# A gate in front of two more head pairs' loads, in a block-sparse attention kernel with a feed-forward layer

## Chip, cores, metric

One Trainium2 chip, one core. The metric is device time of one execution in microseconds (us), the median of several executions. Times within a trace count from the span's start.

## The reference

Attention with a block mask over 4 batches, 8 heads, 768 positions, head size 64, then a layer that multiplies two projections, and two matrices behind it:

```python
scores = scale * np.matmul(q, k.transpose(0, 1, 3, 2))
# mask: neighbours, first and last block, three sampled blocks per row of blocks
scores = np.where(mask, scores, -1000000000.0)
attn = np.exp(scores - np.max(scores, axis=-1, keepdims=True))
attn = attn / (np.sum(attn, axis=-1, keepdims=True) + 1e-09)
attn_out = np.matmul(attn, v)
x = np.ascontiguousarray(attn_out.transpose(0, 2, 1, 3)).reshape(B * S, H * D)
a = x @ w1;  b = x @ w2
out = ((a * b) @ w3) @ w_out
```

Inputs and output are float32.

## The kernel before

The program is planned on the host: a list scheduler (`plan.run()`) with estimated costs puts all tasks in an order, and each engine then runs its own tasks in that fixed order. q, k and v come in by loads that GpSimd issues and that cast to bfloat16. One load carries one of the three for a pair of heads: 192 KB as written.

```python
def load(name, out_of, src, writes, deps=()):
    seq[0] += 1
    t = add(name, {POOL: 0.73}, lambda t: nc.gpsimd.dma_start(out=out_of(), in_=src),
            deps=deps, writes=writes, kind="load", prio=seq[0])
    ...                                     # cut: costs for the scheduler

def load_pair(b, pr, which):
    for tag, src in (("qn", qv), ("kn", kv), ("vn", vv)):
        if tag[0] in which:
            key = (tag, b, pr)
            LD[key] = load(f"ld {key}", lambda key=key: T(*key), src[b][:, 2 * pr:2 * pr + 2],
                           [key], gate(b, pr))
```

The work of attention is cut into 48 units: a batch, a third of the rows, a pair of heads. Batch 0 has units 0 to 11; batch 1 does its pairs 0 and 1 in units 12 to 17 and its pairs 2 and 3 from unit 18 on. A gate is a copy of one element per partition on GpSimd that reads the reciprocal (`rec`) of the unit `lead` = 9 places ahead. GpSimd runs in order, so all loads behind the gate wait too.

```python
def gate(b, pr):
    at = next(i for i, u in enumerate(units) if u[0] == b and u[2] // 2 == pr // 2) - int(PRM["lead"])
    if b < 2 or at < 0:
        return ()
    if at not in GATE:
        ...                                 # cut: names
        GATE[at] = add(f"gate {at}", {POOL: 0.2}, lambda t, rk=rk: nc.gpsimd.tensor_copy(
            gate_sb, T(*rk)[:, 0, 0]), reads=[rk], prio=seq[0])
    return (GATE[at],)
```

For pairs 2 and 3 of batch 1, VectorE copies q and k to another layout (`qs`) and v to a wider tile, and SyncE transposes `qs` by DMA. SyncE's queue also transposes the attention output (`x`) and two blocks of w3 (`w3t`). These transposes and the loads share 16 DMA engines, in two queues: "software" for what GpSimd issues, "hardware" for what SyncE and ScalarE issue.

The softmax here doesn't subtract the row's maximum and nothing guards it: scores larger than these inputs give would overflow.

## Time and profile before

| | before |
|---|---|
| median of the three runs | 244.33 us (244.26 to 244.6) |
| span of the profiled run, granted clock of TensorE | 242.7 us, 1.00 |
| busy: TensorE, ScalarE, VectorE, GpSimd | 98%, 77%, 72%, 18% |
| the six loads concerned: issued, landed | 40.6 to 48.7 us, 57.0 to 64.0 us |
| their first reader, their last reader | 64.2 us, 71.6 us |

A load has three times: its issue on GpSimd, its landing, and the start of its reader. The timeline of GpSimd shows only the first, the DMA view the second (as time since the issue), the timeline of the reading engine the third. The free time between landing and reader is called slack here.

### The profile page before, as it was taken

Reading aid. Unit: us, or ns where it says so; the run is one execution under the profiler, and the core shown is the slowest. Engines: PE = TensorE matmul, PEld = TensorE weight load, DVE = VectorE, ACT = ScalarE, POOL = GpSimd, SP = SyncE. Lnnn points to the kernel's source line nnn. Section 1 sums busy time; section 2 is a strip of 40 time slices with the busy share of each in tenths; the row PEclk is TensorE's granted clock in tenths of the full one; section 3 lists DMA queues with packets and bytes.
Section 4 is the critical chain, followed back from the end, with each engine's and each line's share of the span. In section 5 each row is a group of like instructions: output and inputs, shape, how many; then the busy total and the mean of one; then the engine's idle time right before and its main releaser. Section 6 shows DMA issues by size and latency. Waiting matters only on the chain.

```text
span 242.7 us, 6332 instructions
## 1 busy us (share of the span) xinstructions
PE 237.5 (98%) x2651; PEld 137.8 (57%) x2651; DVE 175.3 (72%) x319; ACT 186.3 (77%) x239; POOL 44.4 (18%) x74
## 2 busy tenths in 40 slices
PE   8999999999999999999999999999999999999995
PEld 7466666667655555555555555554555544444583
DVE  6999898887998787787889778987776831143041
ACT  4898989999889798999899899899989532332341
POOL 9852443410016000700240070000000000000000
PEclk9999999999999999999999999999999999999999
DMA  7999999999869971999199479910024121300312
GB/s 168 182 204 208 207 189 164 193 174 168 121 87 175 174 99 23 113 219 203 58 160 136 111 97 222 201 38 1 26 63 154 24 43 43 130 0 4 130 43 89
DMA packets 52898, 29.39 MB, mean 121 GB/s; under 512 B 32645, under 2 KB 48901, under 8 KB 52869
## 3 DMA queue, kind: packets, MB, share of 16 engines
q0 software_dynamic: 16832, 14.29, 40.9%
q1 hardware_dynamic: 35348, 14.23, 30.3%
q10 hardware_dynamic: 688, 0.46, 0.6%
q8 instruction: 21, 0.34, 0.6%
q14 instruction: 9, 0.07, 0.1%
HBM read 29.36 MB, written 6.29 MB: 147 GB/s over the span
## 4 chain that ended last, share of the span: by engine, by line
PE 91%; DVE 5%; DMA 2%; POOL 1%; issue 0%; POOLq 0%
PE f L748 35%; PE f L774 17%; PE o L665 15%; PE s L639 15%; PE f L728 6%; DMA kn<-in_k_dram 2%; DVE mask L343 1%; DVE e L651 1%; PE f L716 1%; PE f L584 1%; DVE qkt L343 1%; DVE qs L343 1%; POOL qn L379 0%; POOL hotf L414 0%; DVE w3t L343 0%
## 5 line engine op out<-in xcount | busy, mean ns | idle before, releaser
L645 ACT ACTIVATE e<-s 128x1024 bf16<-128x1024 f32 x144 | 140.9, 1025 | 13.5 <-PE s L639 13.1
L748 PE MATMUL f<-x,w 128*128 128x512 bf16 (+1 forms) x448 | 93.7, 349 | 0.0
L651 DVE TENSOR_TENSOR e<-e,mask 128x2048 bf16<-128x2048 bf16 x72 | 87.5, 1219 | 4.9 <-ACT e L645 4.3
L759 DVE TENSOR_TENSOR big<-f,a 128x512 bf16<-128x512 f32 (+1 forms) x56 | 34.2, 612 | 34.5 <-PE f L748 25.5
L748 PEld LDWEIGHTS <-w 128*128 128x128 bf16 x448 | 39.4, 98 | 31.7 <-issue 4.4
L665 PEld LDWEIGHTS <-e 128*128 128x128 bf16 x1152 | 44.6, 97 | 19.9 <-DVE e L651 5.0
L665 PE MATMUL o<-v,e 128*128 128x65 bf16 x1152 | 50.5, 194 | 0.5 <-DVE xn L678 0.5
L756 ACT CAST a<-f 128x512 bf16<-128x512 f32 (+1 forms) x56 | 29.5, 529 | 22.7 <-PE f L748 22.7
L774 PE MATMUL f<-wf,big 128*128 128x512 bf16 (+2 forms) x208 | 46.6, 363 | 0.0
L639 PE MATMUL s<-qkt 64*128 64x256 bf16 x576 | 44.5, 272 | 0.3 <-DVE qkt L343 0.3
L639 PEld LDWEIGHTS <-qkt 64*128 64x128 bf16 x576 | 22.1, 94 | 22.0 <-issue 18.3
L774 PEld LDWEIGHTS <-big 128*128 128x128 bf16 x208 | 17.9, 98 | 17.6 <-issue 1.9
L343 ACT COPY ob<-f 128x512 f32<-128x512 f32 (+1 forms) x20 | 11.6, 578 | 13.1 <-PE f L774 13.1
L678 DVE TENSOR_TENSOR xn<-o,rec 128x256 bf16<-128x256 f32 x48 | 20.3, 423 | 1.2
L673 DVE RECIPROCAL rec<-o 128x4 f32<-128x4 f32 x48 | 8.6, 180 | 16.8 <-PE o L665 16.7
L728 PE MATMUL f<-wo,w3t 128*128 128x512 bf16 x64 | 17.3, 380 | 0.0
L458 POOL COPY gate<-rec 128x1 f32<-128x1 f32 x4 | 0.8, 189 | 76.4 <-DVE rec L673 76.4
L379 POOL DMA_DIRECT2D vn<-in_v_dram x16 | 11.4, 714 | 3.5 <-DVE rec L673 1.0
L379 POOL DMA_DIRECT2D qn<-in_q_dram x15 | 10.9, 725 | 3.5 <-issue 1.6
L379 POOL DMA_DIRECT2D kn<-in_k_dram x15 | 10.8, 717 | 4.1 <-DMA vn<-in_v_dram 1.9
L480 PE MATMUL o<-zero 128*128 128x128 bf16 (+2 forms) x51 | 6.7, 303 | 1.1 <-POOL zero L477 1.1
L728 PEld LDWEIGHTS <-w3t 128*128 128x128 bf16 x64 | 4.9, 98 | 4.3 <-issue 1.7
(64 smaller groups left out, 91.5 us busy)
## 6 DMA issues: line engine op xcount, KB each, us to landing
out_dram<-ob SPq DMA_DIRECT2D x23, 256.0 KB, 2.2
vn<-in_v_dram POOLq DMA_DIRECT2D x16, 192.0 KB, 8.9
qn<-in_q_dram POOLq DMA_DIRECT2D x15, 192.0 KB, 6.3
kn<-in_k_dram POOLq DMA_DIRECT2D x15, 192.0 KB, 7.2
big<-in_moe_w_dram POOLq DMA_DIRECT2D x8, 256.0 KB, 12.0
w<-in_moe_w_dram POOLq DMA_DIRECT2D x4, 512.0 KB, 13.8
wo<-in_moe_w_out_dram POOLq DMA_DIRECT2D x2, 512.0 KB, 11.5
q<-in_q_dram SPq DMA_DIRECT2D x2, 192.0 KB, 3.4
```

Of the source, the lines that this page charges most:

```text
L343: (nc.scalar.copy if t.eng == ACT else nc.vector.tensor_copy)(out, in_)
L379: t = add(name, {POOL: 0.73}, lambda t: nc.gpsimd.dma_start(out=out_of(), in_=src), deps=deps, writes=writes, kind="load", prio=seq[0])
L639: nc.tensor.matmul(s[:, h, k2 * QT:(k2 + 1) * QT], lhsT=z[64 * h:64 * h + 64, 1, kc * 128:(kc + 1) * 128], rhs=z[64 * h:64 * h + 64, 0, t3 ...
L645: exps.append(add(f"E {m} {j}", {ACT: 0.915}, lambda t, sk=sk, ek=ek, j=j: nc.scalar.activation(T(*ek)[:, j], T(*sk), AF.Exp, scale=1.0 / ...
L651: tm = add(f"K {m}", {DVE: 1.137}, lambda t, ek=ek, t3=t3, pick=pick: nc.vector.tensor_tensor(T(*ek), T(*ek), mask[:, t3, pick, :].unsquee ...
L665: nc.tensor.matmul(o[:, qt, h, :], lhsT=e[:, j, h, lo:lo + 128], rhs=w[:, h, kc, :], start=kc == 0 and qt == 0 and h == 0, stop=kc == C - ...
L678: tx = add(f"xn {rk}", {DVE: 0.342}, lambda t, rk=rk, ok=ok, xk=xk, pr=pr: nc.vector.tensor_tensor(T(*xk)[:, :, 128 * pr:128 * pr + 128].r ...
L728: nc.tensor.matmul(T(*key), lhsT=T("w3t", i)[:, j, :], rhs=wo_sb[:, j, :], start=j == 0, stop=j == NF - 1)
L748: nc.tensor.matmul(T(*key)[:, :nt], lhsT=w[:, c, f * 128:(f + 1) * 128], rhs=T(*xk)[:, c, :nt], start=c == 0, stop=c == 3)
L756: ta = add(f"a {i}{f}", {ACT: 0.06 + 0.43 * r}, lambda t, ak=ak, key=ends["w1"][0], nt=nt: nc.scalar.copy(T(*ak)[:, :nt], T(*key)[:, :nt]) ...
L759: nc.vector.tensor_tensor(T(*hk)[:, 512 * (f % 2):512 * (f % 2) + nt], T(*key)[:, :nt], T(*ak)[:, :nt], op=ALU.mult),
L774: nc.tensor.matmul(T(*key)[:, :width], lhsT=T(*hk[f // 2])[:, at:at + 128], rhs=wf_sb[:, f, cols], start=f == 0, stop=f == NF - 1)
```

## The change

The loads of the last two pairs of batch 1 had no gate; batches 2 and 3 have one for each two pairs. The change gives these six loads a gate as well, so that fewer transfers are in flight while weights and transposes compete for the DMA engines.

```diff
-        if b < 2 or at < 0:
+        if b == 0 or b == 1 and pr < 2 or at < 0:
             return ()
```

## The prediction

> **What bounds the kernel now.** I read the page of the kernel before first: the busy shares, then the chain of work that ended last.
>
> ```profile
> span 242.7 us, 6332 instructions
> PE 237.5 (98%) x2651; PEld 137.8 (57%) x2651; DVE 175.3 (72%) x319; ACT 186.3 (77%) x239; POOL 44.4 (18%) x74
> PE 91%; DVE 5%; DMA 2%; POOL 1%; issue 0%; POOLq 0%
> ```
>
> TensorE is busy for 237.5 of 242.7 us and is 91% of the chain that ended last. The 5.2 us that it isn't busy lie before 30 us (8.40 of 10, 9.63 of 10 and 9.84 of 10 us busy in the first three stretches of ten) and after the last matmul. In every stretch between 40 and 90 us, where the change acts, TensorE is busy without a break. DMA in the chain is one load at 3 us. So a change of load times can move the end only if it makes TensorE wait where it doesn't now, or removes a wait that the busy bars hide. I looked for both.
>
> The second view is the timeline of GpSimd, which issues all loads that cast. Columns: start, duration, engine, line, operation, tile, count, then in brackets the idle time before and what ended it.
>
> ```profile
> 39.16 0.74 POOL L379 DMA_DIRECT2D w<-in_moe_w_dram  x1 [0.58 <-DMA qn<-in_q_dram]
> 40.56 0.70 POOL L379 DMA_DIRECT2D qn<-in_q_dram  x1 [0.66 <-DMA kn<-in_k_dram]
> 43.18 0.72 POOL L379 DMA_DIRECT2D kn<-in_k_dram  x1 [1.93 <-DMA vn<-in_v_dram]
> 44.62 0.72 POOL L379 DMA_DIRECT2D vn<-in_v_dram  x1 [0.72 <-DMA big<-in_moe_w_dram]
> 45.97 0.72 POOL L379 DMA_DIRECT2D qn<-in_q_dram  x1 [0.63 <-PE f L584]
> 47.55 0.72 POOL L379 DMA_DIRECT2D kn<-in_k_dram  x1 [0.86 <-PE f L748]
> 48.72 0.72 POOL L379 DMA_DIRECT2D vn<-in_v_dram  x1 [0.46 <-DVE e L651]
> 71.76 0.22 POOL L458 COPY gate<-rec 128x1 f32<-128x1 f32 x1 [22.32 <-DVE rec L673]
> ```
>
> The six q, k, v lines from 40.56 to 48.72 are the loads of pairs 2 and 3 of batch 1, exactly those that the change gates. The line at 39.16 is the load before them, the second half of w2. The line at 71.76 is the first gate as it exists now, for batch 2. The six loads are not free today either: each is held until the eighth load before it has landed. So the software queue is kept eight deep.
>
> The third view gives the landing time, taken over a window that holds one issue at a time (last column: us from issue to landing): w1's second half, w2's second half, then q, k, v of pair 2 and q, k, v of pair 3.
>
> ```profile
> w<-in_moe_w_dram POOLq DMA_DIRECT2D x1, 512.0 KB, 14.6
> w<-in_moe_w_dram POOLq DMA_DIRECT2D x1, 512.0 KB, 16.3
> ...
> qn<-in_q_dram POOLq DMA_DIRECT2D x1, 192.0 KB, 16.4
> kn<-in_k_dram POOLq DMA_DIRECT2D x1, 192.0 KB, 15.1
> ...
> vn<-in_v_dram POOLq DMA_DIRECT2D x1, 192.0 KB, 16.4
> qn<-in_q_dram POOLq DMA_DIRECT2D x1, 192.0 KB, 15.6
> kn<-in_k_dram POOLq DMA_DIRECT2D x1, 192.0 KB, 15.2
> vn<-in_v_dram POOLq DMA_DIRECT2D x1, 192.0 KB, 15.3
> ```
>
> Adding these to the issue times gives landings at 52.4 (w1, issued at 37.82), 55.5 (w2), 57.0, 58.3, 61.0, 61.6, 62.8 and 64.0 us. They come in issue order and one behind the other: w2 takes 3.1 us behind w1, and the six loads take 8.5 us together, 1.4 us each. A load of 192 KB that finds a short queue takes much less from issue to landing: the first one behind the gate at 71.76 took 5.0 us. So of the 15 to 16 us some 10 are time in line. That line is the fact that decides this case.
>
> The fourth view is the timeline of VectorE around the consumers.
>
> ```profile
> 48.71 0.17 DVE L673 RECIPROCAL rec<-o 128x4 f32<-128x4 f32 x1
> ...
> 64.17 0.33 DVE L596 COPY qs<-qn 128x768 bf16<-128x768 bf16 x1
> ...
> 66.16 0.36 DVE L609 COPY v<-vn 128x768 bf16<-128x768 bf16 x1
> ...
> 71.60 0.34 DVE L609 COPY v<-vn 128x768 bf16<-128x768 bf16 x1
> ```
>
> The reciprocal at 48.71 is the tenth of the kernel; it is the one that the new gate reads. The three copies are the first, third and last readers of the six loads; the others are at 64.75, 69.24 and 69.51. None shows idle time waiting for a load. Slack now: 64.17 - 57.0 = 7.2 us for q of pair 2, 64.75 - 58.3 = 6.4 for k, 66.16 - 61.0 = 5.2 for v, 69.24 - 61.6 = 7.6, 69.51 - 62.8 = 6.7 and 71.60 - 64.0 = 7.6 for pair 3.
>
> **What the Trainium skill says.** "DMA: Bandwidth & Descriptors", section "Queues, rings and completion order": each DMA engine takes turns between queue rows at packet granularity, and within a row "descriptors are consumed in ring order". The landings above agree: eight loads, one order. The consequence is that a load cannot slow one that stands ahead of it in its own row; it can only take turns with the other rows, here the transposes that SyncE issues. The same page, section "Issuing engines are not separate DMA queues", says that both kinds run on the same engines; the trace agrees, since a transpose of weights issued at 44.27 took 16.7 us to land, against 3 to 4 us for transposes issued from 64.5 on. "Perfetto Trace Analysis", section "Summary: the profiler window per engine type", says that the slice of a GpSimd DMA leaves out the data movement: 0.72 us on the timeline against 15 to 16 us to landing, so the timeline of GpSimd alone would mislead. "Advanced Engine Details and Errata", section "Mode Summary", says that GpSimd and VectorE share a port and can block each other. That would matter because six issues move. The trace doesn't show it at this size: the mask multiply at 42.43, which the issue at 43.18 overlaps, took 1.22 us, and the one at 50.06, where GpSimd is idle, took 1.22 us too.
>
> **The change part by part.** The gate for this pair of loads is the unit 9 places ahead of unit 18, the first unit that needs them: unit 9, the tenth of 12 in batch 0. The order of instructions, compared between both kernels, is the same on TensorE, VectorE, ScalarE and SyncE; GpSimd has one more instruction, a copy of one element per partition, ahead of the six loads.
>
> Removed: the six separate waits for landings, by then long satisfied (the last load waited for had landed at 34.74 + 13.4 = 48.1 us), and VectorE's waits ahead of the v loads.
>
> Added: one gate copy of about 0.2 us (0.22 in the row at 71.76), on an engine that is 18% busy, and one wait on VectorE before the reciprocal two units later, at 54.98, because the reciprocal's two buffers rotate. The gate will be done by about 49.2, so this costs only the extra semaphore instruction of 0.02 us.
>
> Moved: the reciprocal ends at 48.88. By the gate at 71.76 (reciprocal 71.51, copy 71.76, first load 72.24) the first load follows a reciprocal's start by 0.73 us, so q of pair 2 is issued at about 49.4 and the rest follow 0.72 us apart: 50.2, 50.9, 51.6, 52.3, 53.0. The delays are 8.9, 7.0, 6.3, 5.6, 4.8 and 4.3 us.
>
> What becomes of the delay: at 49.4 the queue still holds w1 until 52.4 and w2 until 55.5. By then five of the six have been issued for over 2.5 us, and the sixth, at 53.0, stands behind the others until 62.8. So the line never runs dry, and the six land when they did: about 57, 58, 61, 62, 63, 64. The delay is taken out of time in line; issue to landing falls to some 7.5, 8, 10, 10, 10.5 and 11 us. Nothing ahead of them is faster: w1, w2 and the transposes face a queue that is as continuously full as before. Sum on the path that sets the end: 0.0 us, with perhaps 0.02 us on VectorE off the path. That is 244.33 + 0 = 244.3 us.
>
> **The rivals.** First, the intended gain: fewer loads in flight between 40 and 49 us give the weights and transposes more bandwidth. For it speaks that the DMA engines are full there. Against it: the gated loads moved no bytes before 55.5, so they took none from anybody. And even if w2 came sooner, TensorE isn't waiting: the order on TensorE is fixed, and the matmuls of the weights run without idle time. The late transpose of weights lands at about 61.0 and is used at 64.1. Worth 0, at most 0.2 us: 244.1 to 244.3.
>
> Second, the delay is passed on in full, if a load needed its whole 15 us whatever the queue holds. Then q of pair 2 lands at 65.9 (1.7 us late for 64.17), k at 65.3 (0.5 late), v at 67.3 (1.1 late), and pair 3 is in time (67.2, 67.6, 68.3 against 69.24, 69.51, 71.60). VectorE would stand idle for at most 1.7 us. It has spare time, but mask multiplies behind it feed TensorE, so up to 1.7 us could reach the end: 246.0. Against it are the 5.0 us behind the existing gate, and the order of landings.
>
> Third, the six issues in one burst from 49.4 to 53.7 collide with VectorE at the shared port. The sign could be either, since they leave 40 to 49 us. Over 4.3 us a slow-down of a tenth would be 0.4 us of VectorE, which has 0.26 to 0.95 us gaps in this stretch: 244.3 to 244.5.
>
> **Range and chances.** The three runs before spread from 244.26 to 244.6. I take 0 for the change, add about 0.5 us on the slow side for a part of the second and third rival, and the same below for run-to-run spread and the first. The predicted time is 244.3 us, the range 243.8 to 244.9 us. Two per cent would be 4.9 us either way, well beyond the 1.7 us of the worst rival: faster 0.01, within 2% 0.98, slower 0.01.
>
> **What would show it right or wrong.** Right: a fifth gate near 49 us after about 9 us of idle time on GpSimd (39.90 to 49), the six issues at 49.4 to 53.0, time to landing of 7 to 11 us, landings within about 1 us of the old ones, and no wait of VectorE for a load at 64 to 72 us. TensorE's busy time stays at 237.5. Wrong: w2 landing clearly before 55.5, a weights transpose much under 16.7 us, or a dip of DMA near 50 us, which would say that the gated loads had taken bandwidth; or an idle line of VectorE in front of the copies at 64.17 to 71.60, which would say that the queue had run dry and the delay was passed on.

## The result

| | before | changed |
|---|---|---|
| median | 244.47 us (244.26 to 245.01, 4 runs) | 244.3 us (244.04 to 244.56, 4 runs) |
| ratio | | 0.999 (95%: 0.9969 to 1.001) |

A ratio here is the mean time of one kernel's fast runs over the mean of the other's from the same rounds, so it isn't quite the ratio of the medians that are quoted. The time did not change.

The page of the changed kernel has nearly the same totals and one more instruction:

```profile
span 242.6 us, 6333 instructions
PE 237.1 (98%) x2651; PEld 137.3 (57%) x2651; DVE 175.3 (72%) x319; ACT 186.4 (77%) x239; POOL 44.6 (18%) x75
PE 91%; DVE 5%; DMA 2%; POOL 1%; issue 0%; POOLq 0%
```

Timeline of GpSimd in the changed kernel (start, duration, engine, line, operation, tile, count, then idle time before and its end):

```profile
48.94 0.22 POOL L458 COPY gate<-rec 128x1 f32<-128x1 f32 x1 [9.03 <-DVE rec L673]
49.17 0.70 POOL L379 DMA_DIRECT2D qn<-in_q_dram  x1
49.87 0.72 POOL L379 DMA_DIRECT2D kn<-in_k_dram  x1
50.58 0.73 POOL L379 DMA_DIRECT2D vn<-in_v_dram  x1
51.29 0.74 POOL L379 DMA_DIRECT2D qn<-in_q_dram  x1
52.00 0.75 POOL L379 DMA_DIRECT2D kn<-in_k_dram  x1
52.71 0.75 POOL L379 DMA_DIRECT2D vn<-in_v_dram  x1
```

GpSimd stands 9.03 us before the gate, then issues the six loads in a row, as predicted within 0.3 us. The last column of the DMA view gives their time to landing:

```profile
qn<-in_q_dram POOLq DMA_DIRECT2D x1, 192.0 KB, 11.2
kn<-in_k_dram POOLq DMA_DIRECT2D x1, 192.0 KB, 11.0
vn<-in_v_dram POOLq DMA_DIRECT2D x1, 192.0 KB, 12.2
qn<-in_q_dram POOLq DMA_DIRECT2D x1, 192.0 KB, 12.6
kn<-in_k_dram POOLq DMA_DIRECT2D x1, 192.0 KB, 13.2
vn<-in_v_dram POOLq DMA_DIRECT2D x1, 192.0 KB, 14.0
```

Here the profile departs from the prediction. Added to the issues, these give 60.4, 60.9, 62.8, 63.9, 65.2 and 66.7 us: 1.8 to 3.4 us later than before, where "the six land when they did" was forecast. The readers on VectorE did not notice:

```profile
64.20 0.33 DVE L596 COPY qs<-qn 128x768 bf16<-128x768 bf16 x1
66.19 0.36 DVE L609 COPY v<-vn 128x768 bf16<-128x768 bf16 x1
71.64 0.33 DVE L609 COPY v<-vn 128x768 bf16<-128x768 bf16 x1
```

They start within 0.04 us of before, with no idle time in front. The smallest slack fell from 5.2 us to 66.19 - 62.8 = 3.4 us in this trace. So the time is as forecast, but one step isn't, and the experiments had two questions: is this stage really off the path, and why do the loads land late?

The lateness shows in the DMA view of one microsecond, 54 to 55 us: queue, packets, MB, share of the 16 engines' time. First before, then changed:

```profile
q0 software_dynamic: 189, 0.14, 89.8%
q1 hardware_dynamic: 192, 0.05, 36.3%
```

```profile
q1 hardware_dynamic: 166, 0.04, 76.6%
q0 software_dynamic: 81, 0.07, 51.2%
```

Before, the two queues move the same number of packets, as they do when they take turns. In the changed kernel the software queue moves half as much, and a hardware packet takes over twice the time: 76.6% of 16 us over 166 packets is 74 ns, against 30 ns before.

### The profile page after: what moved, and what is told of

Same layout as the page of the kernel before. It is cut to its first block, busy times and chain, and to the rows that moved or that the text cites. A ratio compares the mean times of both kernels' runs of the same rounds, so it can differ in the third digit from the quotient of the medians.

```text
span 242.6 us, 6333 instructions
## 1 busy us (share of the span) xinstructions
PE 237.1 (98%) x2651; PEld 137.3 (57%) x2651; DVE 175.3 (72%) x319; ACT 186.4 (77%) x239; POOL 44.6 (18%) x75
## 4 chain that ended last, share of the span: by engine, by line
PE 91%; DVE 5%; DMA 2%; POOL 1%; issue 0%; POOLq 0%
PE f L748 35%; PE f L774 17%; PE o L665 15%; PE s L639 15%; PE f L728 6%; DMA kn<-in_k_dram 2%; DVE mask L343 1%; DVE e L651 1%; PE f L716 1%; PE f L584 1%; DVE qkt L343 1%; DVE qs L343 1%; POOL qn L379 0%; POOL hotf L414 0%; DVE w3t L343 0%
## 5 line engine op out<-in xcount | busy, mean ns | idle before, releaser
L343 ACT COPY ob<-f 128x512 f32<-128x512 f32 (+1 forms) x20 | 11.5, 577 | 13.1 <-PE f L774 13.1
L480 PE MATMUL o<-zero 128*128 128x128 bf16 (+2 forms) x51 | 6.2, 288 | 1.1 <-POOL zero L477 1.1
```

The source lines that it names most:

```text
L343: (nc.scalar.copy if t.eng == ACT else nc.vector.tensor_copy)(out, in_)
```

## The experiments

Eleven runs. A single run of a kernel here had a granted clock of 0.998 or more in the profile. In the runs called "gate at unit n" the order of TensorE, VectorE, ScalarE and SyncE is kept exactly as it was before: the six loads and one gate are moved behind the reciprocal of unit n after scheduling, so only the issue times differ. The edit, with n in the place of 8:

```diff
     log = plan.run()
+    moved = [t for t in log if t.name in [f"ld {(tag, 1, pr)}" for tag in ("qn", "kn", "vn") for pr in (2, 3)]]
+    rk_new = ("rec", *units[8])
+    gate_new = Task("gate new", {POOL: 0.2}, (), (), (), lambda t: nc.gpsimd.tensor_copy(
+        gate_sb, T(*rk_new)[:, 0, 0]), "", 0, "N")
+    gate_new.eng = POOL
+    rest = [t for t in log if t not in moved]
+    at = next(i for i, t in enumerate(rest) if t.name == f"rec {rk_new}") + 1
+    log = rest[:at] + [gate_new] + moved + rest[at:]
```

The landings of all runs with the six loads, in us, each worked out as issue plus time to landing from that run's profile (to 0.1 us; gate9_fill is the disturbed trace told of below, in which all of this lies 3.3 us later):

| run | first issue | q, k, v of pair 2 | q, k, v of pair 3 |
|---|---|---|---|
| reader starts (before) | | 64.2, 64.8, 66.2 | 69.2, 69.5, 71.6 |
| before | 40.6 | 57.0, 58.3, 61.0 | 61.6, 62.8, 64.0 |
| before_again | 40.2 | 56.8, 58.1, 59.7 | 60.9, 62.4, 63.5 |
| gate_unit8 | 45.2 | 57.2, 58.7, 61.4 | 62.2, 63.2, 64.7 |
| changed | 49.2 | 60.4, 60.9, 62.8 | 63.9, 65.2, 66.7 |
| after_again | 49.4 | 60.3, 60.9, 63.5 | 64.5, 65.9, 67.2 |
| after_timed | 49.2 | 60.7, 61.2, 63.7 | 64.8, 66.1, 67.6 |
| gate9_no_w3t7 | 49.1 | 56.1, 57.1, 58.1 | 59.0, 60.4, 61.5 |
| gate9_fill | 52.5 | 63.6, 64.1, 65.2 | 66.6, 68.2, 69.3 |
| gate9_fill_again | 49.1 | 61.6, 62.5, 64.0 | 65.3, 66.6, 68.4 |
| gate_unit11 | 55.8 | 59.8, 63.6, 64.9 | 66.1, 66.5, 67.5 |
| gate_unit12 | 60.0 | 63.4, 64.5, 66.6 | 67.6, 68.7, 71.0 |
| gate_unit13 | 64.7 | 68.2, 69.6, 72.1 | 73.3, 74.4, 75.9 |

### Both kernels once more

> The kernel before, once more, for a second trace. Both theories: the six loads of pairs 2 and 3 of batch 1 land at about 57.0, 58.3, 61.0, 61.6, 62.8 and 64.0 us, within 0.7 us of the first trace; 244.3 us. If they scatter by 2 us or more from trace to trace, the later landings seen in the changed kernel (60.4, 60.9, 62.8, 63.9, 65.2, 66.7) need no cause of their own.

> The changed kernel, once more, for a second trace. Theory A (the later landings are an effect of the gate): last load lands at 66 to 67 us again, and the third load at 62 to 63. Theory B (they are chance): landings scatter between 64 and 67 us. Time 244.3 us either way.

244.5 and 244.64 us, one run each. Before_again differs from the first trace by at most 1.3 us, in one load, where 0.7 was expected; its last load lands at 63.5. After_again lands its third at 63.5 and its last at 67.2, each a little later than the expected 62 to 63 and 66 to 67. Three traces of the change and two of before do not overlap at any of the six loads. The late landing is an effect of the change, not chance.

> The changed kernel against the kernel before, five rounds. Theory P (the end is set by the fixed work of TensorE): ratio 1.000 within 0.0015. Rival (the later landings or the added wait cost something): 1.002 or more.

244.61 us (244.29 to 245.63) against 244.7 us, ratio 1.0003 (0.9985 to 1.002). The expectation of 1.000 within 0.0015 holds; the interval excludes a cost of more than 0.2%, about 0.5 us.

### The loads left out

```diff
+    log = [t for t in log if t.name not in [f"ld {(tag, 1, pr)}" for tag in ("qn", "kn", "vn") for pr in (2, 3)]]
     for t in log:
         t.go(t)
+        if t.name == "ld ('vn', 1, 1)":
+            for tag in ("qn", "kn", "vn"):
+                for pr in (2, 3):
+                    tl[tag, 1, pr] = tl[tag, 1, pr - 2]
```

> The six loads are left out and pairs 2 and 3 of batch 1 read the tiles of pairs 0 and 1: wrong result on purpose, all else in the same order. Theory P (the end is set by the fixed work of TensorE, and no load or transpose between 40 and 70 us is on the path): 244.3 us, within 0.3 of before, though the transposes land several us earlier. Rival Q (bandwidth freed by the loads is worth something, and the change gained it and lost as much by lateness): at least 0.5 us faster than before.

244.55 us, ratio 1.0006 (0.9989 to 1.0023). The transposes did get the bandwidth; the DMA view for the issues at 44 us and at 55 us:

```profile
w3t<-big SPq DMA_TRANSPOSE x1, 12.2
...
x<-xn SPq DMA_TRANSPOSE x1, 2.8
```

Before, these took 16.7 and 8.6 us (a third, `x` issued at 43 us, took 12.6 instead of 11.4). So 4.5 and 5.8 us of faster transposes are worth nothing. This decides against the intended gain: even with the six loads gone, which is more than a gate can do, the kernel takes the same time. By the interval, no delay of the loads in this stage could have paid more than 0.1%, about 0.3 us.

### The gate one unit earlier

> The gate one unit earlier (reciprocal at 44.5 us), orders of TensorE, VectorE, ScalarE and SyncE unchanged. Theory A1 (the gated loads came so late that part of the DMA engines had finished the loads ahead and stood without software work at 53 to 55 us): issued from about 45.1 us there is always software work, so the last load lands at 64.0 us within 0.7, and the software queue keeps about 190 packets in each us from 53 to 57. Theory A2 (it is the gate itself, or six issues in a burst): the last load still lands 2 to 3 us late. Time 244.3 us either way.

244.54 us (one run). Landings return to those of the first trace of before, within 0.7 us. In the microsecond from 54 us:

```profile
q0 software_dynamic: 177, 0.14, 91.4%
q1 hardware_dynamic: 175, 0.04, 38.0%
```

It has the gate and a burst of six issues too, but no dip. So the late landing is not due to the gate as such (A2 falls); it is due to how late the loads are issued.

### The gate two, three and four units later

> The gate two units later than in the change (reciprocal at 55.0 us, loads issued from 55.4 us), orders of the other engines unchanged. Theory P with the slow start seen in the changed kernel (first software packets 5 us after the issue while transposes run): first packets near 60 us, landings about 62, 63.5, 65, 66.5, 68 and 69.5 us, each still ahead of its reader (64.2, 64.8, 66.2, 69.3, 69.5, 71.6); no wait of VectorE over 0.5 us, 244.4 us. Rival (the slack is smaller than read, or bandwidth counts): VectorE waits 1 us or more and the time rises by 0.5 us or more.

244.55 us, ratio 0.9999 (0.9978 to 1.0019), no wait of VectorE for a load. The landings came within 2.5 us of the expectation, mostly earlier; the first load landed in only 4.0 us. The slow start that was expected did not occur: the weights' transpose landed at about 57 us, just as the first gated packets started.

> The gate three units later than in the change (reciprocal at 59.9 us, issues from 60.2 us): the slack of 10 us is then used up. Theory P: with a start after 1.9 us and 1.4 us a load, landings at 65.0, 66.4, 67.8, 69.2, 70.6 and 72.0 us; VectorE waits for the loads for 1.5 to 3 us in all, and part of it reaches TensorE: 245 to 246.5 us. Rival (loads of this stage do not matter at all, VectorE's spare time takes it): 244.4 us.

244.99 us (244.18 to 245.49), ratio 1.0011 (0.9989 to 1.0032): the same within noise, though two of its four runs are above 245.3. VectorE had one wait for these loads in its list of waits:

```profile
DVE v L609 <- DMA vn<-in_v_dram: 0.5, 1, 0.5
```

The expected 245 to 246.5 us was too high: the loads landed 3.4 to 7.5 us after issue (no packet of the hardware queue ran from 60 to 68 us), and 0.5 us of waiting leaves no trace in the time. A whole 20 us of later issue, from 40 to 60 us, costs nothing measurable.

> The gate four units later than in the change (reciprocal at 64.1 us, issues from 64.4 us), where the last slack must be gone: in the kernel with the gate at the thirteenth unit VectorE waited 0.5 us for a load. Theory P: landings near 67.9, 68.5, 70.5, 72, 73 and 75 us against readers from 64.2 us on; VectorE waits 3.5 to 6 us for loads, TensorE then shows idle time that it has nowhere between 40 and 90 us now, and the kernel takes 246 to 250 us. Rival (this stage has so much spare time that TensorE's end does not move): 244.4 to 245 us.

250.84 us (250.03 to 251.57), ratio 1.0256 (1.0227 to 1.0285): slower, and a little over the expected range. Here the slack is gone. Waits, 60 to 80 us (engine and group that waited, what released it: us in total, times, longest):

```profile
DVE qs L596 <- DMA qn<-in_q_dram: 3.9, 1, 3.9
PE o L665 <- DVE xn L678: 3.8, 1, 3.8
DVE v L609 <- DMA vn<-in_v_dram: 1.0, 1, 1.0
DVE qs L596 <- DMA kn<-in_k_dram: 0.7, 1, 0.7
```

And the busy time from 65 to 75 us (us, busy time of TensorE, weight loads, VectorE, ScalarE, GpSimd, then TensorE's granted clock, DMA share, GB/s):

```profile
65.00:70.00 5.00, 1.22 (x18) 0.93 (x18) 1.06 (x4) 1.00 (x2) 3.92 (x6) 0.91 0.81 100
70.00:75.00 5.00, 4.95 (x42) 2.34 (x42) 3.99 (x8) 2.53 (x3) 0.00 (x0) 0.75 1.29 149
```

VectorE waits 3.9 + 0.7 + 1.0 = 5.6 us for loads. A normalisation (`xn`) that the value matmuls need stands behind them in VectorE's fixed order, so TensorE stands too, busy 1.22 of 5 us where it was busy 5.00. Its granted clock is 0.75 in the next five. The last of the six readers starts at 77.07 us instead of 71.60. The profiled execution's span is 5.4 us longer (248.1 against 242.7 us), the median 6.3 us. TensorE's wait is 3.8 us of that; its mean granted clock was 0.993 in this execution and 0.986 to 0.993 in the others, against 1.00 before, and how much of the rest is the clock was not taken apart. So a late load does reach the end once the slack is gone: 5.6 us of VectorE's waiting shows, 0.5 us did not, and nothing between was measured. The slack ends between these two gates, whose first issues are 4.7 us apart (60.0 and 64.7 us).

### Why late: the transpose taken away

```diff
+    for t in log:
+        if t.name == "xw 7":            # the DMA transpose of weight rows 7
+            t.go = lambda t: nc.gpsimd.memset(T("w3t", 7), 0.0)
```

This is the change with the gate at unit 9, made by the same edit. Its output is wrong, which doesn't matter for the time.

> The change as it is, but the transpose of weight rows 7, in flight from 44 to 60 us, is replaced by a fill with zeros (wrong result on purpose). Theory H (the gated loads start late because the transposes take the DMA engines as soon as the software queue is empty): from 53 to 55 us the software queue keeps 150 packets or more in each us, and the last load lands by 64.5 us. Theory S (a load started on a nearly empty software queue needs 5 us whatever else runs): a dip below 80 software packets in some us between 52 and 56 stays, and the last load lands after 65 us. Time 244.3 us either way.

244.39 us (one run). The six loads land at 56.1 to 61.5 us, and from 54 to 55 us the software queue has the engines to itself:

```profile
q0 software_dynamic: 272, 0.20, 130.0%
```

Theory S falls. Same gate, same issue times within 0.1 us, same work ahead in the software queue, and no late start. In this one trace against three, the transpose is needed for the effect.

### Why late: more work ahead

```diff
+    fill_sb = fixed("fill", [128, 4, d_ff // 2], BF16)
+    fill = Task("fill", {POOL: 0.7}, (), (), (), lambda t: nc.gpsimd.dma_start(
+        out=fill_sb, in_=moe_w2.rearrange("(c r) f -> r c f", r=128)[:, :, d_ff // 2:]), "", 0, "N")
+    fill.eng = POOL
+    at = next(i for i, t in enumerate(log) if t.name == "wh w2 1") + 1
+    log = log[:at] + [fill] + log[at:]
```

This, too, is the change with the gate at unit 9, made by the same edit.

> The change as it is, with one more load of 512 KB, which nobody reads, issued behind w2 at about 40.5 us, so that the software queue still has work when the gated loads come. Theory E (an empty software queue is what lets the transposes in and makes the gated loads start late): no dip, 170 packets or more of the software queue in each whole us from 53 to 57 except where all packets pause, and although 512 KB more are moved (about 3.3 us at the rate of 0.15 MB a us), the last load lands at 66 to 68 us, no later than in the changed kernel. Theory G (the gate or the burst causes the late start by itself): a dip after the extra load is done, and the last load lands at 69 to 71 us. Time 244.3 to 244.6 us either way, since the readers wait from 64.2 us on at most a us.

244.65 us, ratio 0.9998 (0.9982 to 1.0015), but the profiled execution took 247.67 us: TensorE's granted clock was 0.67 from 10 to 15 us, and everything after it lay 3.3 us later, the gate and the six issues included, while the extra load did not. There was a dip from 54 us and a last landing at 69.3 us. In this trace the first engines were done with the extra load at 54.5 us, only 2 us after the first gated issue, so that it could not cover a start of 5 us, and the trace decides nothing. By the letter of the expectation it spoke for G.

> The kernel with the extra load once more, since its profiled execution was disturbed (TensorE's clock fell to 0.67 between 10 and 15 us and all of it came 3.3 us later, the gated loads too, so that the extra load was done on half of the DMA engines 2 us after their issue). Theory E (an empty software queue lets the transposes in and makes the gated loads start late): with the gate at 49 us the extra load covers the 5 us that the gated loads need to start; 150 software packets or more in each us from 53 to 57, last load at 66 to 68 us. Theory G (the gate or the burst by itself): a us with fewer than 100 software packets between 53 and 59, without a pause of all packets, and the last load at 69 us or later. Time 244.3 to 244.7 us.

Undisturbed: 244.31 us (one run). No dip; from 54 to 55 us:

```profile
q0 software_dynamic: 155, 0.16, 91.9%
```

The software queue moved 155 to 190 packets in each microsecond from 53 to 59. The last load landed at 68.4 us, a little over the expected 66 to 68, though 512 KB more had to be moved first: only 0.8 to 1.7 us later than in the changed kernel's three traces. E holds, in one trace.

### What these add up to

The trace records the size of each packet, and packets of 768 bytes belong to q, k and v loads alone. The first of them behind the gate start about 5 us after the first issue in the changed kernel: at 54.3 us in its first trace, 54.6 in after_again, 53.9 in after_timed. With the DMA engines nearly idle it is 1.4 us: at 57.2 us in gate_unit11 and at 61.3 us in gate_unit12. Without the weights' transpose they start at 52.9 us, 3.8 us after the first issue, as soon as w2 is done on the first engines.

So most of the 5 us is still time in line behind w2: against the run without the transpose, the start is some 1 to 1.5 us later (4.7 to 5.2 us after the first issue against 3.8). Time in line is not the whole of it, though. In gate9_fill the first engines were done with the load ahead 2 us after the first gated issue, and the first gated packet still came 5.0 us after it, at 57.5 us.

The engines do not finish w2 together: its packets thin out from 53.0 us and the last run at 55.5 us. An engine that is done early has in the changed kernel no gated load to go on with until 54 to 55 us, and turns to transposes alone: from 53 to 54 us the software queue moves 102 packets and the hardware queue 382, against 183 and 182 before. In before, in gate_unit8 and with the extra load, the next load is there.

What the runs do not settle is why the gated loads are not there when the first engines run out of other loads while that transpose is in flight, and why transpose packets then take 74 ns on average.

## Why the prediction was right or wrong

- **The bound.** Right. TensorE is busy without a break from 40 to 90 us in both kernels, and taking the six loads away altogether changed nothing (1.0006).
- **The orders.** Right: one more instruction, on GpSimd, and GpSimd issues from 49.17 us where 49.4 was worked out.
- **"So the line never runs dry, and the six land when they did."** This step failed. The reading took one queue as one line that ends at 55.5 us, when w2 lands. That is the end on the slowest DMA engine; the faster ones were done 2.5 us earlier. The sentence of the skill that the prediction quotes begins "On each SDMA engine": it gives an order for each engine, not one line for all 16. (It stands in a paragraph on the queues of SyncE and ScalarE; that GpSimd's queue keeps an order too is what the eight landings show.) And the prediction took 2.5 us as ample time for an issued load to start; with a transpose in flight it took about 5, of which up to 3.8 were spent behind w2. Issue to landing was 11.0 to 14.0 us instead of the 7.5 to 11 forecast, and landings moved by 1.8 to 3.4 us in the first trace instead of under 1.
- **"Nothing ahead of them is faster."** Nearly right: the weights' transpose took 15.7 us instead of 16.7, w2 landed at 56.0 instead of 55.5. The transposes of `x` became slower: the one issued at 43 us took 13.1 us instead of 11.4, the one at 55.7 us 10.2 instead of 8.6. So one transpose became 1.0 us faster and two became 1.6 to 1.7 us slower. The prediction named a dip of DMA near 50 us as a sign against it. A dip of the software queue came, at 53 to 58 us, but not for the reason given there: not because the loads had taken bandwidth before, but because their own start was late.
- **The slack.** This saved the number. It was 5.2 us or more, the error used up 1.8 to 3.4 of it, and 3.4 us remained (2.5 in after_timed, the least of the three traces). So the right number does not confirm the step above: issued 6.6 us later still, in gate_unit11, the loads left the time the same as well.
- **The second rival** (the delay is passed on). Its mechanism is real, as gate_unit13 shows, and it is what happened here in part, within the slack. Its size of 246.0 us was for a case that never came near: gate_unit12, issued 10.8 us later still, waits 0.5 us and costs nothing measurable. (Two of its sums are 0.1 us high: 49.4 + 16.4 is 65.8, 52.3 + 15.2 is 67.5.)
- **The first rival** (bandwidth). It is worth nothing: no_loads freed more than any gate can. But one argument against it was wrong, "the gated loads moved no bytes before 55.5": in the kernel before, their first packets of 768 bytes run at 52.8 us, on engines that are done with w2. The evidence that loads and transposes share engines was weak as well, since it compared transposes of different tiles (those from 64.5 us on, 2.7 to 4.3 us); no_loads shows it on one and the same, 12.2 us against 16.7.
- **The third rival** (the shared port). The mask multiply that starts at 50.05 us, under the moved issues, took 1.22 us, as without them. The skill's sentence speaks of VectorE instructions in the modes that use both ports, which the prediction left out, and no view here tells whether the mask multiply is one. But no VectorE instruction between 49.1 and 54.5 us took over 0.01 us longer than before, the copies at 49.78, 51.19 and 53.87 us (0.35, 0.35 and 0.36 us) among them. No run was made for it alone.

## What to carry to other kernels

Here, delaying loads in a queue that is served in order gave nothing to what stands ahead of them, and shortening a transfer gave nothing while its reader came late in a fixed order: read slack from landing to reader first, and test the bound by leaving the transfer out. Judge "the queue still has work" by the first DMA engine that is done, not by the landing, which is the last one's, and keep several microseconds of issued work ahead when DMA transposes run beside. Here a gate at unit 8, 9, 11 or 12 cost nothing measurable and only unit 13 cost time, 2.6%; a gate that pays nothing brings the kernel nearer to that edge.

## What the Trainium skill lacked or had wrong

- "DMA: Bandwidth & Descriptors", section "Latency and other measured facts", gives about 1 us to the first byte for a load issued by GpSimd. With nearly idle DMA engines these runs come near (1.4 us from the start of the issue, which itself takes 0.7 us). With a DMA transpose in flight it was about 5 us in four traces (4.7 to 5.2), of which in three up to 3.8 us were time in line, but in gate9_fill only about 2. The page doesn't say that this can happen.
- The same page, section "Queues, rings and completion order", describes turns between queues at packet granularity. The kernel before agrees (189 and 192 packets in one us). In the changed kernel it was 81 and 166 in the same us, when not all engines had a gated load yet, and 121 and 129 two us later. What the page doesn't tell is that a transpose packet then takes 74 ns on average instead of 30. Why stays open.
- "DMA: Bandwidth & Descriptors" says that the engines of one load finish independently and that two of the 16 are usually slower, but no page that I found says by how much: w2 was done on the first engines at 53.0 us and landed at 56.0 in the changed kernel.
